# Moving seven of nine feature tiles of an attention gate from TensorE rows to VectorE multiply-adds in a one-core transformer block

## The chip, the core and the metric

The kernel runs on one core of a Trainium2 chip. The metric is the device time of one execution in microseconds (us); lower is better. A core has five engines with a queue of instructions each, which run side by side and wait for one another through semaphores: TensorE (PE, matrix multiplies; PEld is its weight load), VectorE (DVE), ScalarE (ACT), GpSimd (POOL) and SyncE (SP, which here only starts transfers). Transfers between HBM and the on-chip memory SBUF are done by 16 DMA engines. TensorE writes to PSUM, eight banks of 512 f32 values in each of 128 partitions.

## What is computed

One block of a diffusion transformer, on 2 batches of 256 tokens with 1152 features, all in bf16:

```
mod = (silu(c) @ w_mod).reshape(B, 6, 1, D)
shift_a, scale_a, gate_a, shift_m, scale_m, gate_m = [mod[:, i] for i in range(6)]
h = layernorm(x) * (1 + scale_a) + shift_a
q, k, v = (h @ wqkv) split in three, two heads of 576
attn = softmax(q @ k^T * 576 ** -0.5)
a = (attn @ v) @ wo
x = x + gate_a * a
h2 = layernorm(x) * (1 + scale_m) + shift_m
out = x + gate_m * (gelu(h2 @ w_fc1) @ w_fc2)
```

`c` is one vector of 1152 for each batch, so each of the six vectors of `mod` is a product of two rows with a matrix of 1152 x 1152. The change is about `gate_a`, a vector of 1152 for each batch that multiplies the output of the attention projection.

## The kernel before

**Recording and ordering.** The kernel records units of work, each for one engine with an estimated duration (`Sched`, L172), and finds the dependences between them from the memory that they read and write. `schedule` (L281) then fixes the order of each engine's queue with a model of the times. TensorE and SP keep the order in which they were recorded. VectorE, ScalarE and GpSimd take, of the units that the model has ready, the one with the longest path behind it; the first units of VectorE and ScalarE are written out by hand (L909). The order is fixed when the program is built: on the chip an engine waits at the head of its queue, even if what stands behind it is ready.

**Stages.** All 512 tokens lie in SBUF as feature tiles of 128 partitions, KT = 9 of them. TensorE's order is:

- the scale part of `mod` and the K projection (to about 30 us), then `sh` (L887 to L889), the row of `shift_a`
- the last K tile (`proj` to tile 17), and six of nine Q tiles at once, feature tile by feature tile, in PSUM banks 2 to 6 and 1 (L1104 to L1108); the other three Q tiles by `proj` (L871) in banks 0, 1 and 2
- for each batch b and head h, of number idx = 2b + h: the scores in one bank (`s_bank`, L919) and the softmax behind it (`s_and_softmax`, L931): on VectorE `smax` (row maximum, L943), `snb` (L944), `sri` (reciprocal, L949) and `spn` (the normalising multiply, L951), on ScalarE two `sexp` (exponential, L947)
- the V projection in 12 tiles of 128 tokens x 384 features, in banks 0, 1, 2 in turn (`v_proj`, L965). They stand between the score and transpose stages: `PT_b_h` (L953) transposes the probabilities of (b, h) and needs its `spn`; `PT_ev` copies them out of the bank
- `rows` (L977), after the V tile v_2_0: the three vectors `gate_a`, `shift_m` and `scale_m`
- the rest of V, attention times V (`pv`), the output projection `wo_tile` (L1055), the transposes of the second layer norm (`xn2_T`, L1077), and the two MLP matrices to the end

**Row products.** `quad_mm` (L880) has the two rows of silu(c) as weights and streams a weight matrix past them, with the 32-column groups dealt over four parts of the array (q = 0 to 3), so that four matmuls of n columns each stand for 4n columns. `sh` makes nine passes of 288 columns. `rows` makes for each of nine feature tiles one pass of 448 columns into bank 3 and one of 416 into bank 4 (`row_parts`, L975): 27 groups of 32 for each part, 9 for each vector. ScalarE then copies the gate rows to ROWS (`rows_ev`), VectorE transposes the other two vectors (`mt_0`, `mt_1`, L985; `sc1m`, L987), and GpSimd's queue stores the gate in HBM (`st_g0`, `st_g1`) and reads it back to all 128 partitions as GA[b] (`ld_g0`, `ld_g1`, L991). `wo_tile` multiplies by GA[b] (`wo_t1`, VectorE, L1067), adds x on GpSimd (L1068), and goes on to the statistics (L731, L734, L735, L1072) and the normalised tile `xn2` on ScalarE (L1073), which `xn2_T` needs. `wo_tile` and the MLP take the banks 2, 3, 4, 5, 0, 1 in turn.

**The gate of the MLP** is made in another way, late in the kernel, under the MLP's matmuls (`mlp_gate`, L994): VectorE multiplies the weight tile by silu(c), one value for each partition, and adds up over the nine feature tiles (L999 for the first, L1002 for the others); then it sums over the partitions by a 32 x 32 transpose (L1006), a reduction (L1008), three copies (L1011), three additions (L1014), a copy to bf16 (L1016) and a transpose (L1017). GpSimd clears a small tile for it (L1005), stores the result and reads it back to all partitions.

**Loads.** SP's queue holds all weight loads in order: the nine WQ tiles; WV, which overlays the weights of `sh` and so waits for `sh`; the three parts of WMODR (weights of `rows`, three vectors wide, L891); WO; the first two tiles of w_fc1; after the last V tile two more; the weights of the MLP gate (`ld_gm`, into the region O_R); and w_fc2.

**Evictions.** PSUM is copied to SBUF by ScalarE (L681) or VectorE (L683); `qk_evac` (L867) and `v_proj` (L972) take them in turn.

Of the kernel before, what the change touches and what calls it, by code (L numbers as in the profile page):

```python
# [506 lines left out]
CH = 384  # L507
NCH = 3
F0 = 8
KC = 5  # L510
KG = 6


def c_mm(n):
# [7 lines left out]
def c_dve_psum32(n):  # L522
    return 110.0 + 1.13 * n
# [18 lines left out]
def build_kernel(nc, x, c, wqkv, wo, w_mod, w_fc1, w_fc2, out):  # L542
    S = Sched()
# [3 lines left out]
    scratch = scratch_t.ap()  # L547
    with (
# [20 lines left out]
        W1 = 20736  # L569
        O_A, O_B, O_C, O_R = 0, W1, 2 * W1, 3 * W1  # L570
# [25 lines left out]
        WMODR = wmat(O_R + W1, 3 * D)  # L596
# [18 lines left out]
        GA = [sb(O_GA + b * 2304, 2304) for b in range(2)]  # L615
        GM = [sb(o + 18432, 2304) for o in (O_A, O_C)]
        XN2 = [sb(O_R + 4 * W1 - (i + 1) * 2304, 2304) for i in range(4)]
        ROWS = sb(O_R + 4 * W1 - 5 * 2304, 2304)[:, 0:288]
        T1 = [sb(O_X + i * 1536, 1536, F32) for i in range(3)]
        OST = [sb(O_X + 4608 + i * 768, 768) for i in range(3)]  # L620
        gt_offs = ([O_P + i * 1024 for i in range(8)] + [O_B + i * 1024 for i in range(20)]
# [11 lines left out]
        ST32 = sb(misc(72), 72, F32)  # L633
# [4 lines left out]
        MT = sb(misc(2304), 2304, F32)  # L638
# [21 lines left out]
        wmod_v = w_mod.rearrange("(k p) f -> p k f", p=P)  # L660
# [34 lines left out]
        for (ka, kb) in ((0, KC), (KC, KT)):  # L695
            w = (kb - ka) * P
# [49 lines left out]
        for t in range(4):  # L746
# [3 lines left out]
            else:  # L750
# [3 lines left out]
                                                                                 op0=ALU.subtract, op1=ALU.mult),  # L754
# [112 lines left out]
        def qk_evac(j, bank):  # L867
            copy_on("act" if ev_rr[0] % 2 == 0 else "dve", QK[:, j, :], ps32(bank), 512, False, "qk_ev%d" % j)
            ev_rr[0] += 1

        def proj(W, j, dst_j, H, bank):  # L871
            S.unit("pe", KT * c_mm(512), "qk_%d" % dst_j)
            for kt in range(KT):
                mm(ps32(bank), W[:, kt, j * 128:(j + 1) * 128], H[:, kt, :], kt == 0, kt == KT - 1)
            qk_evac(dst_j, bank)

        def quads(w, g0, g1, q):
            return w.rearrange("p (g q c) -> p g q c", q=4, c=32)[:, g0:g1, q, :]
# [8 lines left out]
        S.unit("pe", KT * 4 * 31.0 + 100.0, "sh")  # L887
        for kt in range(KT):
            quad_mm(0, WSH[:, kt, :], 0, 9, kt)  # L889
        dma(WV, wqkv_v[:, :, 2 * D:3 * D], D * D * 2, "ld_wv", run=2304)  # L890
        for k0 in range(0, KT, 3):  # L891
            dma(WMODR[:, k0:k0 + 3, :], wmod_v[:, k0:k0 + 3, 2 * D:5 * D], 3 * P * 3 * D * 2, "ld_modr%d" % k0)
        MT1 = ps32(0, 0, 288)
        dve(c_dve_psum32(288), lambda e: e.transpose(SHA, MT1), [MT1], [SHA], "sha")  # L894
        for kt in range(KT):
            for b in range(2):
                src, dst = HK[:, kt, b * 256:(b + 1) * 256], HX[:, kt, b * 256:(b + 1) * 256]
# [77 lines left out]
        row_parts = ((3, 0, 14), (4, 14, 27))  # L975

        def rows():  # L977
            S.unit("pe", KT * 864 / 2.4 + 500.0, "rows")
# [3 lines left out]
            copy_on("act", ROWS, ps32(3, 0, 288), 288, False, "rows_ev")  # L982
            for i, (bank, c0, n, d0) in enumerate(((3, 288, 160, 0), (4, 0, 416, 160))):
                src, dst = ps32(bank, c0, n), MT[:, d0:d0 + n]
                dve(c_dve_psum32(n), lambda e, src=src, dst=dst: e.transpose(dst, src), [src], [dst], "mt_%d" % i)  # L985
            sc, so = MT[:, 288:576].rearrange("p (k r) -> p k r", r=32)[:, :, 0:2], SC1M.rearrange("p (k b) -> p k b", b=2)
            dve(170, lambda e: e.tensor_scalar(out=so, in0=sc, scalar1=1.0, scalar2=None, op0=ALU.add), [sc], [so], "sc1m")  # L987
            for b in range(2):
                dma(scratch[0, b].rearrange("(k q c) -> q k c", q=4, c=32), ROWS[b:128:32, :].rearrange("p (k c) -> p k c", c=32),
                    2304, "st_g%d" % b, eng="pool")  # L990
            for b in range(2):  # L991
                dma(GA[b], scratch[0, b].partition_broadcast(P), P * D * 2, "ld_g%d" % b, eng="pool")

        def mlp_gate(prev):  # L994
            for b in range(2):
# [117 lines left out]
        s_halves()  # L1113
# [57 lines left out]
        for t in range(4):  # L1171
            b = t // 2
# [69 lines left out]
```

## Time and profile before

| | |
|---|---|
| time, median of 3 runs | 246.3 us (246.1 to 247.2) |
| the profiled execution | 246.26 us, of which the profile's span is 244.2 us and 2.06 us lie around it |
| TensorE busy | 239.3 us (98%) |
| VectorE, ScalarE, GpSimd busy | 98.7 us (40%), 63.0 us (26%), 21.5 us (9%) |
| DMA | 51.57 MB, mean 211 GB/s |
| granted TensorE clock | 1.0 of full speed |

All times in the text are from the start of the span. An "idle before" is the time an engine stood still in front of an instruction, and its releaser is what ended the wait. The lines of the MLP gate, L999 to L1017, are the nearest rows for the operations that the change adds. The timeline merges neighbouring instructions of one line; the start of a merged row is that of its first.

### The profile page before, as it was taken

Reading aid. Unit: us, or ns where it says so; the run is one execution under the profiler, and the core shown is the slowest. Engines: PE = TensorE matmul, PEld = TensorE weight load, DVE = VectorE, ACT = ScalarE, POOL = GpSimd, SP = SyncE. Lnnn points to the kernel's source line nnn. Section 1 sums busy time; section 2 is a strip of 40 time slices with the busy share of each in tenths; the row PEclk is TensorE's granted clock in tenths of the full one; section 3 lists DMA queues with packets and bytes.
Section 4 is the critical chain, followed back from the end, with each engine's and each line's share of the span. In section 5 each row is a group of like instructions: output and inputs, shape, how many; then the busy total and the mean of one; then the engine's idle time right before and its main releaser. Section 6 shows DMA issues by size and latency. Waiting matters only on the chain.

```text
span 244.2 us, 3973 instructions
## 1 busy us (share of the span) xinstructions
PE 239.3 (98%) x1721; PEld 146.8 (60%) x1731; DVE 98.7 (40%) x205; ACT 63.0 (26%) x128; POOL 21.5 (9%) x37
## 2 busy tenths in 40 slices
PE   7999999999999999999999999999999999999995
PEld 2689844466557666798544444444565656566575
DVE  3742450446323689879999600000022222111112
ACT  5730340235312306983322333222000000000000
POOL 1400000000021275600000110000000000000000
DMA  6999999999994999979943589200000000000000
GB/s 244 350 377 393 389 381 401 419 422 406 387 329 111 341 386 391 392 246 396 349 132 101 172 256 393 79 0 3 0 16 16 19 17 16 19 16 16 29 22 16
DMA packets 28875, 51.57 MB, mean 211 GB/s; under 512 B 1587, under 2 KB 15675, under 8 KB 28859
## 3 DMA queue, kind: packets, MB, share of 16 engines
q1 hardware_dynamic: 28384, 50.14, 56.9%
q0 software_dynamic: 448, 1.19, 2.0%
q8 instruction: 13, 0.21, 0.4%
q14 instruction: 3, 0.02, 0.0%
q10 hardware_dynamic: 27, 0.00, 0.0%
HBM read 50.14 MB, written 1.19 MB: 210 GB/s over the span
## 4 chain that ended last, share of the span: by engine, by line
PE 97%; ACT 1%; issue 0%; DVE 0%; POOL 0%; POOLq 0%
PE psum L686 95%; PE psum L689 2%; ACT arena L1091 1%; ACT arena L1073 1%; DVE arena L792 0%; POOL arena L709 0%; DVE arena L1184 0%; DVE arena L1185 0%; POOL arena L708 0%; DVE arena L783 0%; POOL arena L713 0%; POOLq L1227 0%
## 5 line engine op out<-in xcount | busy, mean ns | idle before, releaser
L686 PE MATMUL psum<-arena 128*128 128x384 bf16 (+9 forms) x1632 | 236.1, 312 | 2.2 <-POOL arena L709 1.4
L686 PEld LDWEIGHTS psum<-arena 128*128 128x128 bf16 (+1 forms) x1642 | 141.4, 97 | 92.3 <-issue 5.0
L1184 DVE TENSOR_TENSOR arena<-psum,arena 128x384 f32<-128x384 f32 (+3 forms) x14 | 7.0, 501 | 89.4 <-PE psum L686 89.4
L1101 ACT ACTIVATE arena<-psum 128x512 bf16<-128x512 f32 (+1 forms) x44 | 22.5, 522 | 42.6 <-PE psum L686 42.6
L681 ACT ACTIVATE arena<-psum 128x512 bf16<-128x512 f32 (+6 forms) x28 | 14.8, 549 | 40.1 <-PE psum L686 38.2
L683 DVE CAST arena<-psum 128x512 bf16<-128x512 f32 (+2 forms) x21 | 13.0, 627 | 26.5 <-PE psum L686 26.3
L1002 DVE SCALAR_TENSOR_TENSOR arena<-arena 128x1152 f32<-128x1152 bf16 x16 | 21.3, 1409 | 0.0
L1068 POOL TENSOR_TENSOR arena<-arena 128x384 f32<-128x384 f32 x12 | 11.0, 914 | 12.9 <-DVE arena L1067 11.7
L667 POOL DMA_DIRECT2D dit_scratch<-arena x4 | 2.6, 662 | 94.0 <-ACT arena L681 58.7
L731 DVE BATCH_NORM_STATS2 arena<-arena 128x6 f32<-128x384 f32 (+1 forms) x18 | 9.5, 549 | 1.2 <-DMA arena<-in_x_dram 1.1
L1073 ACT ACTIVATE arena<-arena 128x1152 bf16<-128x1152 f32 x4 | 5.4, 1353 | 9.5 <-DVE arena L1072 9.5
L1067 DVE TENSOR_TENSOR arena<-psum,arena 128x384 f32<-128x384 f32 x12 | 6.6, 548 | 3.2 <-PE psum L686 3.0
L689 PEld LDWEIGHTS psum<-arena 128*128 128x128 bf16 (+1 forms) x89 | 6.0, 98 | 2.4 <-DMA arena<-in_c_dram 0.8
L689 PE MATMUL psum<-arena 128*128 128x128 bf16 (+1 forms) x89 | 7.3, 219 | 0.1
L1185 DVE TENSOR_TENSOR arena<-arena 128x384 bf16<-128x384 f32 (+3 forms) x14 | 7.0, 501 | 0.5
L1091 ACT ACTIVATE arena<-psum,arena 128x128 bf16<-128x128 bf16 x16 | 6.1, 460 | 3.2 <-PE psum L689 2.5
L1088 DVE TENSOR_SCALAR arena<-psum,arena 128x128 bf16<-128x128 bf16 x20 | 5.5, 336 | 2.0 <-PE psum L689 1.8
L943 DVE TENSOR_REDUCE arena<-psum 128x2 f32<-128x512 f32 x4 | 2.8, 692 | 4.0 <-PE psum L686 3.7
L947 ACT ACTIVATE arena<-psum,arena 128x256 bf16<-128x256 f32 x8 | 3.7, 470 | 2.4 <-DVE arena L944 1.9
L735 POOL TENSOR_TENSOR arena<-arena 128x1 f32<-128x1 f32 x6 | 3.3, 555 | 6.1 <-DVE arena L734 6.1
L792 DVE TENSOR_SCALAR arena<-psum,arena 128x256 bf16<-128x256 bf16 x7 | 2.4, 348 | 3.6 <-PE psum L689 2.3
L900 ACT ACTIVATE arena<-arena 128x256 bf16<-128x256 bf16 x6 | 2.5, 495 | 3.3 <-DVE arena L894 3.3
(46 smaller groups left out, 43.1 us busy)
## 6 DMA issues: line engine op xcount, KB each, us to landing
arena<-in_w_mod_dram SPq DMA_DIRECT2D x4, 2592.0 KB, 20.2
arena<-in_w_fc_dram SPq DMA_DIRECT2D x9, 1152.0 KB, 8.2
arena<-in_w_fc_dram SPq DMA_DIRECT2D x4, 2592.0 KB, 17.4
arena<-in_wqkv_dram SPq DMA_DIRECT2D x18, 288.0 KB, 10.2
arena<-in_w_mod_dram SPq DMA_DIRECT2D x3, 864.0 KB, 13.2
arena<-in_wqkv_dram SPq DMA_DIRECT2D x1, 2592.0 KB, 10.9
arena<-in_wo_dram SPq DMA_DIRECT2D x1, 2592.0 KB, 32.7
arena<-in_w_mod_dram SPq DMA_DIRECT2D x3, 480.0 KB, 6.8
```

The source lines that it names most:

```text
L681: act(c_act(n), lambda e: e.activation(out=dst, in_=src, func=ACTF.Copy), [src], [dst], name)
L683: dve(c_dve_psum16(n) if psum16 else c_dve_psum32(n), lambda e: e.tensor_copy(dst, src), [src], [dst], name)
L686: S.instr(lambda e: e.matmul(o, lhsT=l, rhs=r, start=st, stop=sp, **kw), reads=[l, r], writes=[o])
L689: S.instr(lambda e: e.transpose(o, i_, idn), reads=[i_, idn], writes=[o])
L731: dve(550, lambda e, s=s, o=o: e.bn_stats(out=o, in_=s), [s], [o], "bn_%s_%d" % (tag, ci))
L1002: u = dve(1300, lambda e, o=o, w=w, s1=s1: e.scalar_tensor_tensor(out=o, in0=w, scalar=s1, in1=o, op0=ALU.mult, op1=ALU.add), [w, s1, o], ...
L1068: S.op("pool", 930, lambda e, xs=xs, x1c=x1c: e.tensor_tensor(out=x1c, in0=x1c, in1=xs, op=ALU.add), reads=[x1c, xs], writes=[x1c], name=" ...
L1073: act(1344, lambda e: e.activation(out=xn2, in_=x1, func=ACTF.Identity, scale=rs, bias=nm), [x1, rs, nm], [xn2], "xn2_%d" % t)
L1091: act(440, lambda e, o=o, dst=dst, s1=s1, s2=s2: e.activation(out=dst, in_=o, func=ACTF.Identity, scale=s1, bias=s2), [o, s1, s2], [dst], ...
L1101: act(c_act(ntok), lambda e: e.activation(out=dst, in_=o, func=ACTF.Gelu_apprx_tanh), [o], [dst], "gelu_%d_%d" % (f, tok0))
L1184: dve(c_dve_psum32(w), lambda e, o=o, gm=gm, t1=t1: e.tensor_tensor(out=t1, in0=o, in1=gm, op=ALU.mult), [o, gm], [t1], "fc2_t1_%d_%d" % ( ...
L1185: dve(c_dve_32(w), lambda e, t1=t1, x1c=x1c, ost=ost: e.tensor_tensor(out=ost, in0=t1, in1=x1c, op=ALU.add), [t1, x1c], [ost], "fc2_out_%d ...
```

## The change

`gate_a` is split: its first NG = 7 feature tiles of 128 (FG = 896 of 1152 features) are made on VectorE in the way of the MLP gate, and the last two stay in `rows`.

- `rows` makes a pass of 352 and one of 288 columns for each feature tile. ROWS, its copy and its store hold 64 columns for each part, and `mt_0` and `mt_1` are 288 columns each.
- `attn_gate` is recorded before the Q tiles: for each feature tile and batch one multiply or multiply-add of 128 x 896 (2 and 16), two transposes and two reductions of 128 x 896, eight small operations on 32 partitions, a clearing of a small tile on GpSimd, and two stores on GpSimd's queue. Its tiles lie in O_R, where `ld_gm` loads later.
- The gate's part of WMODR is loaded by three transfers of its own, of 672 KB each, ahead of WV; the other three WMODR loads shrink from 2592 to 1920 KB.
- All twelve V evictions, and all nine Q evictions but two (`qk_ev1`, `qk_ev3`), go to ScalarE. Before, ScalarE had six of V and four of Q.

In the order of the built program, VectorE's queue has the 18 multiplies and adds spread from the end of the `hx` operations (L903) to behind the last `spn`: seven ahead of `qk_ev1`, four ahead of the first `smax`, then singly between the softmax operations, and the last two behind `spn_3`, followed by the transposes, `ga_red0`, `mt_0`, `mt_1`, `ga_red1` and the small operations. On ScalarE the eviction `qk_ev8` stands ahead of the first `sexp`, and `v_ev1_0` ahead of the last pair. On GpSimd the clearing of the small tile stands near the start, between the clearing at L713 and the making of the identity (L709); the stores are followed by the two reads `ld_g0` and `ld_g1`. TensorE's order is the same but for the widths in `rows`.

```diff
+NG = 7
+FG = NG * 128
...
-        ROWS = sb(O_R + 4 * W1 - 5 * 2304, 2304)[:, 0:288]
+        ROWS = sb(O_R + 4 * W1 - 5 * 2304, 2304)[:, 0:288 - 32 * NG]
+        ACCA = sb(O_R, FG * 8, F32).rearrange("p (b d) -> p b d", b=2)
+        ACTA = sb(O_R + FG * 8, FG * 8, F32).rearrange("p (b d) -> p b d", b=2)
...
-            qk_evac(dst_j, bank)
+            if dst_j == 17:
+                qk_evac(dst_j, bank)
+            else:
+                copy_on("act", QK[:, dst_j, :], ps32(bank), 512, False, "qk_ev%d" % dst_j)
...
+        for k0 in range(0, KT, 3):
+            dma(WMODR[:, k0:k0 + 3, 0:FG], wmod_v[:, k0:k0 + 3, 2 * D:2 * D + FG], 3 * P * FG * 2, "ld_ga%d" % k0, run=FG * 2)
         dma(WV, wqkv_v[:, :, 2 * D:3 * D], D * D * 2, "ld_wv", run=2304)
         for k0 in range(0, KT, 3):
-            dma(WMODR[:, k0:k0 + 3, :], wmod_v[:, k0:k0 + 3, 2 * D:5 * D], 3 * P * 3 * D * 2, "ld_modr%d" % k0)
+            dma(WMODR[:, k0:k0 + 3, FG:3 * D], wmod_v[:, k0:k0 + 3, 2 * D + FG:5 * D], 3 * P * (3 * D - FG) * 2, "ld_modr%d" % k0)
...
-            copy_on("act" if v_rr[0] % 2 else "dve", V[:, t, ci * CH:(ci + 1) * CH], o, CH, False, "v_ev%d_%d" % (t, ci))
+            copy_on("act", V[:, t, ci * CH:(ci + 1) * CH], o, CH, False, "v_ev%d_%d" % (t, ci))
-        row_parts = ((3, 0, 14), (4, 14, 27))
+        row_parts = ((3, NG, 18), (4, 18, 27))
...
+        def attn_gate():
+            for kt in range(KT):
+                for b in range(2):
+                    o, w, s1 = ACCA[:, b, :], WMODR[:, kt, 0:FG], ST32[:, b * 9 + kt:b * 9 + kt + 1]
+                    if kt == 0:
+                        dve(150 + FG * 0.6, lambda e, o=o, w=w, s1=s1: e.tensor_scalar(out=o, in0=w, scalar1=s1, scalar2=None, op0=ALU.mult),
+                            [w, s1], [o], "ga_%d_%d" % (b, kt))
+                    else:
+                        dve(150 + FG * 1.1, lambda e, o=o, w=w, s1=s1: e.scalar_tensor_tensor(out=o, in0=w, scalar=s1, in1=o, op0=ALU.mult, op1=ALU.add),
+                            [w, s1, o], [o], "ga_%d_%d" % (b, kt))
+            pool(100, lambda e: e.memset(GBA, 0.0), [], [GBA], "gba0")
...
+            for b in range(2):
+                dma(scratch[0, b, 0:FG].rearrange("(g c) -> g c", c=32), GTA[0:4 * NG, 32 * b:32 * b + 32], FG * 2, "st_ga%d" % b, eng="pool")
...
+        attn_gate()
         qb = (2, 3, 4, 5, 6, 1)
...
-        for j in range(KG):
-            qk_evac(j, qb[j])
+        for j, eng in ((5, "act"), (1, "dve"), (2, "act"), (3, "dve"), (4, "act"), (0, "act")):
+            copy_on(eng, QK[:, j, :], ps32(qb[j]), 512, False, "qk_ev%d" % j)
```

More of the change, by code (lines that the diff above doesn't have):

```diff
@@ L971, in v_proj @@
                 mm(o, HX[:, kt, t * 128:(t + 1) * 128], WV[:, kt, ci * CH:(ci + 1) * CH], kt == 0, kt == KT - 1)
-            copy_on("act" if v_rr[0] % 2 else "dve", V[:, t, ci * CH:(ci + 1) * CH], o, CH, False, "v_ev%d_%d" % (t, ci))
-        row_parts = ((3, 0, 14), (4, 14, 27))
+            copy_on("act", V[:, t, ci * CH:(ci + 1) * CH], o, CH, False, "v_ev%d_%d" % (t, ci))
+        row_parts = ((3, NG, 18), (4, 18, 27))
         def rows():
-            S.unit("pe", KT * 864 / 2.4 + 500.0, "rows")
+            S.unit("pe", KT * (864 - 32 * NG) / 2.4 + 500.0, "rows")
             for kt in range(KT):
@@ L981, in rows @@
                     quad_mm(bank, WMODR[:, kt, :], g0, g1, kt)
[L982 to L985, printed above, removed]
+            n = 288 - 32 * NG
+            copy_on("act", ROWS, ps32(3, 0, n), n, False, "rows_ev")
+            for i, (bank, c0) in enumerate(((3, n), (4, 0))):
+                src, dst = ps32(bank, c0, 288), MT[:, i * 288:(i + 1) * 288]
+                dve(c_dve_psum32(288), lambda e, src=src, dst=dst: e.transpose(dst, src), [src], [dst], "mt_%d" % i)
             sc, so = MT[:, 288:576].rearrange("p (k r) -> p k r", r=32)[:, :, 0:2], SC1M.rearrange("p (k b) -> p k b", b=2)
@@ L988, in rows @@
             for b in range(2):
-                dma(scratch[0, b].rearrange("(k q c) -> q k c", q=4, c=32), ROWS[b:128:32, :].rearrange("p (k c) -> p k c", c=32),
-                    2304, "st_g%d" % b, eng="pool")
+                dma(scratch[0, b, FG:D].rearrange("(k q c) -> q k c", q=4, c=32), ROWS[b:128:32, :].rearrange("p (k c) -> p k c", c=32),
+                    2304 - 2 * FG, "st_g%d" % b, eng="pool")
             for b in range(2):
                 dma(GA[b], scratch[0, b].partition_broadcast(P), P * D * 2, "ld_g%d" % b, eng="pool")
+        def attn_gate():
[10 more added lines that the diff above has]
+            for b in range(2):
+                a_, t_ = ACCA[:, b, :], ACTA[:, b, :]
+                dve(150 + FG * 1.1, lambda e, a_=a_, t_=t_: e.transpose(t_, a_), [a_], [t_], "ga_T%d" % b)
+                t3, o = t_.rearrange("p (g r) -> p g r", r=32), GPA[:, 0, b, :]
+                dve(150 + FG * 1.1, lambda e, t3=t3, o=o: e.tensor_reduce(out=o, in_=t3, axis=AX.X, op=ALU.add), [t3], [o], "ga_red%d" % b)
+            gp = GPA.rearrange("p q b g -> p q (b g)")
+            for q in range(1, 4):
+                i_, o_ = gp[32 * q:32 * q + 32, 0, :], gp[0:32, q, :]
+                dve(200, lambda e, i_=i_, o_=o_: e.tensor_copy(o_, i_), [i_], [o_], "ga_mv%d" % q)
+            for a_, b_ in ((0, 1), (2, 3), (0, 2)):
+                x_, y_ = gp[0:32, a_, :], gp[0:32, b_, :]
+                dve(200, lambda e, x_=x_, y_=y_: e.tensor_tensor(out=x_, in0=x_, in1=y_, op=ALU.add), [x_, y_], [x_], "ga_add%d" % b_)
+            g0, gb = GPA[0:32, 0, :, :], GBA.rearrange("p (b g) -> p b g", b=2)[:, :, 0:4 * NG]
+            dve(200, lambda e: e.tensor_copy(gb, g0), [g0], [gb], "ga_bf")
+            dve(200, lambda e: e.transpose(GTA, GBA), [GBA], [GTA], "ga_t")
+            for b in range(2):
+                dma(scratch[0, b, 0:FG].rearrange("(g c) -> g c", c=32), GTA[0:4 * NG, 32 * b:32 * b + 32], FG * 2, "st_ga%d" % b, eng="pool")
```

3 lines of the change are left out of this document (added).

## The prediction

> **What bounds the kernel now.** I read the page's busy line first, then what TensorE waits for, then TensorE's work by shape, then the stretch around the change in the timeline. The page and TensorE's waits:
>
> ```profile
> PE 239.3 (98%) x1721; PEld 146.8 (60%) x1731; DVE 98.7 (40%) x205; ACT 63.0 (26%) x128; POOL 21.5 (9%) x37
> ```
>
> ```profile
> PE psum L686 <- POOL arena L709: 1.4, 1, 1.4
> PE psum L686 <- issue: 0.2, 1, 0.2
> ```
>
> TensorE is busy for 239.3 of 244.2 us, and its only real wait is the 1.4 us for the identity at the start. So the end moves by what is taken from TensorE's queue, less each wait that is put into it. VectorE's 40% is an average: what counts is whether it has room between 35 and 82 us. TensorE's weight loads around the two stages with 2-column weights show what a pass costs:
>
> ```profile
> 29.95 0.96 PEld L686 LDWEIGHTS psum<-arena 128*2 128x2 bf16 x36 [0.21 <-issue]
> 31.16 0.33 PEld L686 LDWEIGHTS psum<-arena 128*128 128x128 bf16 x3 [0.25 <-issue]
> ```
>
> ```profile
> 65.96 3.02 PEld L686 LDWEIGHTS psum<-arena 128*2 128x2 bf16 x72 [0.32 <-issue]
> 69.35 0.60 PEld L686 LDWEIGHTS psum<-arena 128*128 128x128 bf16 x5 [0.37 <-issue]
> ```
>
> The first pair is `sh`: nine passes of 288 columns from 29.95 to 31.16, 1.21 us. The second is `rows`: nine passes of 448 and nine of 416, 7776 columns, from 65.96 to 69.35, 3.39 us.
>
> **What is taken away: rows.** After the change there are nine passes of 352 and nine of 288, 5760 columns, 2016 fewer. If what is not streaming is fixed for a stage, a column costs (3.39 - 1.21) / (7776 - 2592) = 0.42 ns, and 0.85 us go. If it is paid by the pass (18 against 9), 3.39 - 2 x 1.21 = 0.97 us are for 2592 columns, 0.37 ns each, and 0.75 us go. I take the middle, **-0.8 us**. Everything behind `rows` on TensorE moves forward together, as it has no wait there.
>
> **The added VectorE work, and its cover.** The nearest rows by shape, and where VectorE meets TensorE:
>
> ```profile
> L1002 DVE SCALAR_TENSOR_TENSOR arena<-arena 128x1152 f32<-128x1152 bf16 x16 | 21.3, 1409 | 0.0
> ...
> L1006 DVE STREAM_TRANSPOSE arena<-arena 128x2304 f32<-128x2304 f32 x1 | 2.6, 2578 | 0.0
> L1008 DVE TENSOR_REDUCE arena<-arena 128x72 f32<-128x2304 f32 x1 | 2.6, 2553 | 0.0
> ...
> L999 DVE TENSOR_SCALAR arena<-arena 128x1152 f32<-128x1152 bf16 x2 | 1.5, 809 | 0.0
> ```
>
> ```profile
> 50.38 0.69 DVE L943 TENSOR_REDUCE arena<-psum 128x2 f32<-128x512 f32 x1 [2.77 <-PE psum L686]
> ...
> 64.03 0.37 PEld L689 LDWEIGHTS psum<-arena 128*128 128x128 bf16 x4
> ...
> 82.71 0.56 DVE L1067 TENSOR_TENSOR arena<-psum,arena 128x384 f32<-128x384 f32 x1 [0.31 <-PE psum L686]
> ```
>
> The 16 multiply-adds of L1002 overlap: they fill 21.35 us, 1.33 us from start to start. For 896 instead of 1152 elements that is 1.05 us (1.04 in proportion; 1.12 with no overlap, by the slope between 558 ns for the 384-element L1185 and 1409 ns). The plain multiplies start 0.77 us apart, 0.6 us at 896. VectorE's queue then runs so:
>
> - Start: the last WQ load is issued at 25.67 and lands 10.0 us later, at 35.7; WV is issued at 31.47 and lands after 10.9, at 42.4. So WV's 2592 KB took 6.7 us, and a gate load of 672 KB, next in the queue, 1.7 us: the three land near 37.4, 39.2 and 40.9.
> - Two multiplies and five adds from 37.4 end at 43.9, before the Q banks are ready at 44.97. Two evictions of 0.66 end at 46.3, four adds at 50.5. `smax_0` could start at 50.38: 0.1 us late.
> - One add more, then `snb_0` at 52.2 (51.11 before); ScalarE has `qk_ev8` until 52.9 (0.60 from 52.32) ahead of the exponentials anyway, and a pair of them takes 1.0 (59.72 to 60.73). `smax_1` waits for TensorE at 55.53, so VectorE catches up there. Going on with 1.05 for each add and the softmax rows' own 0.15 to 0.69, `spn_0` ends at 55.1, `spn_2` at 58.1, `spn_1` at 60.7. TensorE needs them at 59.0, 60.7 and 62.3: slack 3.9, 2.6, 1.6.
> - `spn_3`: ScalarE evicts v_1_0 from 61.02 and then does the last exponentials, to 62.5; `sri_3` to 62.7; `PT_ev1` cannot start before 62.93 and takes 0.42; `spn_3` takes 0.69 and ends at 64.0. TensorE loads its result at 64.03. This is the one tight place: a wait from nothing to 0.3 us. I take **+0.1**.
>
> Behind `spn_3` come two adds, two transposes (by the slope to 619 ns for 416 elements, 1.1 each), two reductions (1.1 each), two transposes of 288 (0.48, the L894 row), 0.13 for `sc1m` and eight small operations, which took 1.80 (136.60 to 138.40): VectorE is done near 73.4, long before its next eviction at 77.97.
>
> **The gate's way through HBM.** The stores took 1.7 to 4.5 us to land, the reads 4.1 to 7.3 (page part 6 and the DMA view by window). GA[0] then lands between 73.4 + 1.7 + 4.1 = 79.2 and 73.4 + 4.5 + 7.3 = 85.2; before, it was 75.09 + 4.1 = 79.2. The DMA engines are nearly empty from 74 to 76 us (share 0.01), so I expect some 80. `wo_t1` needs it at 82.71 - 0.65 = 82.1. A late gate costs nothing at first: TensorE fills six banks, VectorE has 0.90 + 0.44 + 0.44 + 0.16 us of waits to catch up in, and `xn2_0` ends at 92.98 for a weight load at 94.05, 1.07 more. Only past 85.1 does each us cost one. **0**.
>
> **The other edits.** V and Q evictions on ScalarE take 0.49 and 0.60 against 0.56 and 0.69 on VectorE, and a V tile comes every 1.46 to 1.68 us: cover enough, **0**; without it v_2_0 would wait for bank 0, whose eviction ends at 61.5 for a need at 64.4. WV lands 5.2 us later, at 47.6, for a need at 53.2 (eviction at 54.66 less nine matmuls of 0.16). WMODR's last load lands at 34.90 + 26.5 = 61.4 as before, since the bytes ahead are the same, for a need at 66.0. `ld_gm` now waits for the gate's stores (75 to 78), behind the w_fc1 loads in SP's queue and ahead of w_fc2, which is used after 170 us: **0**.
>
> The clearing on GpSimd lands ahead of the identity, TensorE's one wait. Its like (L1005) took 0.17 us, that at L713 0.10 and starts while L708 still runs: 0 to 0.15 later, of which TensorE's later waits before 12 us may swallow some (a weight load stands 0.23 for a transfer at 10.46). **+0.05**.
>
> **A rule weighed.** The Trainium skill, "DMA: Bandwidth & Descriptors", § Bandwidth, advises batches of at least 1 MiB for 75% of peak, against this cut, and § Anatomy of one DMA fits 2.0 us plus bytes over 436 GB/s to one transfer of GpSimd's queue. By it, as an estimate, the three gate loads would take 10.7 us instead of 5.2. The trace speaks against it on SP's queue: the nine WQ loads of 288 KB land at 390 GB/s, as fast as the large ones. What it would do is the third rival.
>
> **Sum.** Against the profiled execution of 246.26 us (its span 244.2 and 2.06 around it; the median is 246.3, so the two may be taken as one): 246.26 - 0.8 + 0.1 + 0.05 = **245.6 us**, a span of 243.6. What a measurement of this kernel can tell from no change is about 0.5%, 1.2 us; my -0.65 is within it.
>
> **Rivals.**
> 1. *The softmax takes the gain back.* VectorE has some 20 changes of operation between 44.97 and 64 us; if each costs 0.05 to 0.1 more for a semaphore than its row shows, `spn_3` is 0.4 to 1.2 late past its slack. For: the 0.0 us of slack there. Against: the waits at 55.53 and 62.93 let VectorE catch up. 245.6 + 0.4 to 1.2: **246.0 to 246.8**. 0.14.
> 2. *The gate lands late, and the time ends above before.* The place is `wo_t1`, the point 85.1 us. The longest store and read give 85.2; if VectorE's tail (27 instructions behind `smax_0`) is also 2.5 us late, 87.7, 2.6 past the point: 245.6 + 2.6 = **248.2**. The old time is passed from 85.8. For: both transfers in series after VectorE's last operation. Against: empty DMA engines at that moment. 0.07.
> 3. *The cut loads leave gaps.* WMODR's last part lands at 61.4 plus the gaps and is needed at 66.0, WV at 47.6 plus the gaps for 53.2; gaps of 5.6 us cost 1.0: **246.6**. Against: no such gap behind the WQ loads. 0.03.
> 4. *The rows do not shrink*, because the 36 narrower pairs of load and matmul are bound by issue: 72 weight loads filled 3.02 us. Against: in `sh` 36 filled 0.96. 246.26 + 0.15, **246.4**. 0.05.
>
> My forecast has 0.69; 0.02 are left for something faster that I do not see.
>
> **Range and chances.** The forecast's own range is 245.2 to 246.0 (wait 0 to 0.3, columns 0.75 to 0.85, start 0 to 0.15, and the spread of the runs, 246.1 to 247.2). To hold 8 in 10 it must take in rivals 1, 3 and 4: 245.1 to 246.9. Faster by over 0.5% (below 245.0): 0.03. Slower by over 0.5% (above 247.5): rival 2 and a tail, 0.08. Within: 0.89.
>
> **What would show it.** `rows`: first to next weight load 2.5 to 2.65 us. Softmax: TensorE's weight load of PT_1_1 with no wait, or one of up to 0.3 with L951 as releaser. Gate: the second pair of stores issued near 73.4, the reads landing before 82, L1067 still released by TensorE. Start: the first matmul at 1.42 to 1.57. I am wrong if TensorE shows waits above 0.5 us between 44 and 100 us, or if VectorE's adds are much longer than 1.05 us apart where nothing stands between them.

## The result, and the profile after

Against the kernel before, run beside it on the same chip, the changed kernel takes **0.9952 [0.9941, 0.9964]** of the time: medians of eleven runs each, 245.35 us (244.78 to 245.97) and 246.71 us (246.1 to 247.51). By this ratio it is 1.2 us less (0.9 to 1.5); the two medians lie 1.36 apart, because this set of the kernel before lies high (its later medians are 246.3 to 246.4). The forecast was 245.6 us in a range of 245.1 to 246.9, a gain of 0.65. The time has two parts: the median span is 243.6 us, where the forecast had 243.6 and the kernel before has 244.3 to 244.4; what lies around the span is 1.75 us, where the kernel before has 2.07 (2.05 to 2.07).

The busy line of the changed kernel's page:

```profile
PE 238.6 (98%) x1721; PEld 146.7 (60%) x1731; DVE 116.8 (48%) x226; ACT 67.0 (27%) x137; POOL 22.4 (9%) x40
```

VectorE has 18.1 us more to do, ScalarE 4.0, TensorE 0.7 less. What TensorE waits for (total, times, longest, in us):

```profile
PE psum L693 <- POOL arena L716: 1.5, 1, 1.5
PE psum L696 <- DMA arena<-in_c_dram: 0.6, 1, 0.6
PE psum L693 <- issue: 0.2, 1, 0.2
```

The second line is new and is no term of the sum: the vector c landed late in this execution. That is why its span is 244.2 us, that of the profile of before, though the median is 0.7 below. Four of the profiles of the experiments, e3, e6_4us, e7 and e11, show c late too (2.73 to 3.07 us), the others do not (2.38 to 2.54, but for e8, where c is loaded behind other work); whether the change has a part in that is not shown. The place is the weight load of c's transpose at the start. Before:

```profile
2.38 0.10 PEld L689 LDWEIGHTS psum<-arena 18*128 18x128 bf16 x1 [0.84 <-DMA arena<-in_c_dram]
```

After:

```profile
3.15 0.10 PEld L696 LDWEIGHTS psum<-arena 18*128 18x128 bf16 x1 [1.54 <-DMA arena<-in_c_dram]
```

It is 0.77 us late at c, 0.75 at the next stage (8.76 for 8.01), and 0.82 at `rows`. To compare the two profiles ahead of `rows`, 0.82 us are to be taken off the times of the changed kernel. The timeline of the changed kernel from the multiply-adds to the stage behind `rows` (start, duration, engine, line, operation, shapes; in brackets the idle time before it and what ended it):

```profile
38.36 5.40 DVE L1015 SCALAR_TENSOR_TENSOR arena<-arena 128x896 f32<-128x896 bf16 x5
...
51.24 0.68 DVE L955 TENSOR_REDUCE arena<-psum 128x2 f32<-128x512 f32 x1
...
64.08 0.68 DVE L963 TENSOR_TENSOR arena<-arena 128x512 bf16<-128x512 bf16 x1
...
64.84 0.37 PEld L696 LDWEIGHTS psum<-arena 128*128 128x128 bf16 x4
...
66.78 2.27 PEld L693 LDWEIGHTS psum<-arena 128*2 128x2 bf16 x72 [0.32 <-issue]
...
69.33 24.63 PEld L693 LDWEIGHTS psum<-arena 128*128 128x128 bf16 x166 [0.28 <-issue]
```

`rows` begins at 66.78 and the next stage at 69.33: 2.55 us for 3.39. Before, they began at 65.96 and 69.35. So the stage gives back what the late c cost, and from there both profiles show the same times to within 0.03 us. From the start of `rows` to the end of the span it is 178.24 us before and 177.42 after. In the second line, 51.24 less 0.82 is 50.42: the first softmax row starts 0.04 later than before, though the multiply-adds stand ahead of it in VectorE's queue. The tight place holds: the last normalised row, L963, ends at 64.76, and TensorE's load of its transpose follows at 64.84 with no wait in brackets. The margin is only 0.08 us.

The groups of the added VectorE work (count, busy us, mean ns of one, idle before):

```profile
L1015 DVE SCALAR_TENSOR_TENSOR arena<-arena 128x896 f32<-128x896 bf16 x16 | 17.6, 1145 | 0.0
...
L1020 DVE STREAM_TRANSPOSE arena<-arena 128x896 f32<-128x896 f32 x2 | 2.1, 1086 | 0.0
L1022 DVE TENSOR_REDUCE arena<-arena 128x28 f32<-128x896 f32 x2 | 2.1, 1043 | 0.0
```

Five adds that follow one another without a break fill 5.40 us, from 38.36 on: less the 1.145 us of the last, that is 1.06 from start to start for the 1.05 of the forecast. The gate's way through HBM, in the same timeline:

```profile
73.79 1.09 POOL L674 DMA_DIRECT2D dit_scratch<-arena  x2 [2.31 <-DVE arena L1032]
...
76.04 1.02 SPq L674 DMA_DIRECT2D arena<-in_w_fc_dram  x2
...
76.39 1.12 POOL L674 DMA_DIRECT2D arena<-dit_scratch  x2 [1.51 <-DMA dit_scratch<-arena]
...
83.28 0.56 DVE L1109 TENSOR_TENSOR arena<-psum,arena 128x384 f32<-128x384 f32 x1 [0.91 <-DMA arena<-dit_scratch]
...
94.02 0.65 PEld L696 LDWEIGHTS psum<-arena 128*128 128x128 bf16 x9
```

The second pair of stores is issued at 73.79, the reads at 76.39, 2.6 us later, and the gate is there 6.9 us after that, at 83.28. VectorE stands idle for 0.91 us ahead of its first user, L1109; 0.31 of these it waited for TensorE in the kernel before too, so the gate is 0.6 us late. TensorE shows no wait behind it: the lateness is swallowed.

### The profile page after: what moved, and what is told of

Its sections match the earlier page's. It is cut to its first block, busy times and chain, and to the rows that moved or that the text cites. A ratio compares the mean times of both kernels' runs of the same rounds, so it can differ in the third digit from the quotient of the medians.

```text
span 244.2 us, 4012 instructions
## 1 busy us (share of the span) xinstructions
PE 238.6 (98%) x1721; PEld 146.7 (60%) x1731; DVE 116.8 (48%) x226; ACT 67.0 (27%) x137; POOL 22.4 (9%) x40
## 4 chain that ended last, share of the span: by engine, by line
PE 96%; ACT 1%; DMA 1%; DVE 0%; issue 0%
PE psum L693 94%; PE psum L696 2%; DMA arena<-in_c_dram 1%; ACT arena L1133 1%; ACT arena L1115 1%; DVE arena L799 0%; DVE arena L1227 0%; DVE arena L1228 0%; DVE arena L790 0%
## 5 line engine op out<-in xcount | busy, mean ns | idle before, releaser
L693 PE MATMUL psum<-arena 128*128 128x384 bf16 (+8 forms) x1632 | 235.3, 310 | 2.2 <-POOL arena L716 1.5
L688 ACT ACTIVATE arena<-psum 128x512 bf16<-128x512 f32 (+6 forms) x37 | 18.9, 539 | 38.4 <-PE psum L693 38.4
L1015 DVE SCALAR_TENSOR_TENSOR arena<-arena 128x896 f32<-128x896 bf16 x16 | 17.6, 1145 | 0.0
L690 DVE CAST arena<-psum 128x512 bf16<-128x512 f32 (+1 forms) x12 | 7.7, 647 | 13.3 <-PE psum L693 13.2
L674 POOL DMA_DIRECT2D dit_scratch<-arena x6 | 3.6, 606 | 96.1 <-ACT arena L688 58.5
L1109 DVE TENSOR_TENSOR arena<-psum,arena 128x384 f32<-128x384 f32 x12 | 6.6, 548 | 2.9 <-PE psum L693 1.8
```

What stands on the lines that cost most here:

```text
L693: S.instr(lambda e: e.matmul(o, lhsT=l, rhs=r, start=st, stop=sp, **kw), reads=[l, r], writes=[o])
L1015: dve(150 + FG * 1.1, lambda e, o=o, w=w, s1=s1: e.scalar_tensor_tensor(out=o, in0=w, scalar=s1, in1=o, op0=ALU.mult, op1=ALU.add), [w, s1 ...
```

## The experiments

My theory: the narrower `rows` alone makes the change of the span, the rest is covered, and the cover of the gate ends at one point, some 3 us past its need. The rivals: the evictions give the gain; the added VectorE work takes something back; the cut loads or the clearing move the start; and, for the cover, that the point lies elsewhere or that lateness past it costs something other than one for one. Times are medians, ratios are to the kernel before with 95% intervals, "around" is the time less the span.

| run | ratio | time | span | around |
|---|---|---|---|---|
| before | | 246.3 to 246.7 | 244.3 to 244.4 | 2.07 |
| after | 0.9952 [0.9941, 0.9964] | 245.35 | 243.6 | 1.75 |
| e1_rows | 0.9968 [0.9957, 0.9979] | 245.58 | 243.6 | 2.07 |
| e2_evict | 0.9997 [0.9989, 1.0006] | 246.33 | 244.2 | 2.09 |
| e3_fullrows | 0.9991 [0.9982, 1.0] | 246.19 | 244.4 | 1.75 |
| e4_clear_late | 0.9949 [0.9937, 0.9961] | 245.07 | 243.3 | 1.76 |
| e5_loads | 0.9993 [0.998, 1.0006] | 246.05 | 244.15 | 1.81 |
| e8_c_later | 0.9955 [0.9939, 0.9971] | 245.23 | 243.5 | 1.74 |
| e6_gate_2us | 1.0009 [1.0, 1.0019] | 246.58 | 244.9 | 1.75 |
| e6_gate_4us | 1.0187 [1.0157, 1.0216] | 250.68 | 248.95 | 1.77 |
| e7_ng8 | 1.0248 [1.0229, 1.0266] | 252.44 | 250.7 | 1.75 |
| e10_gate_sp | 0.9959 [0.9946, 0.9973] | 245.29 | 243.5 | 1.72 |
| e11_ng8_sp | 0.9951 [0.9935, 0.9967] | 245.14 | 243.4 | 1.74 |
| e12_split | 0.9991 [0.9982, 1.0] | 246.15 | 244.25 | 1.83 |

### e1_rows: the narrow rows alone

The kernel before, with `rows` cut and nothing put in its place: the seven tiles of the attention gate are left out, and the store sends other data in their stead.

```diff
-        row_parts = ((3, 0, 14), (4, 14, 27))
+        row_parts = ((3, NG, 18), (4, 18, 27))
...
+                dma(scratch[0, b:b + 1, 0:FG], X[b:b + 1, 0, 0:FG], 2 * FG, "st_ga%d" % b, eng="pool")
```

> The kernel before with the narrow rows alone: no multiply-adds, no cut loads, evictions as before. The first seven tiles of the attention gate are left out (values of x stand in for them). Rows theory: 5760 instead of 7776 columns take 0.85 us out of TensorE's queue and nothing else matters, so the time is 0.85 us below before, and the first to next weight load of rows is 2.55 us. Rival (part of the measured -1.2 us comes from the evictions, the loads or the start): no more than -0.85 here, while one of the other runs shows the rest of about 0.4.

Measured: 0.9968 [0.9957, 0.9979], span 243.6. TensorE's weight loads:

```profile
65.88 2.27 PEld L688 LDWEIGHTS psum<-arena 128*2 128x2 bf16 x72 [0.32 <-issue]
68.42 2.55 PEld L688 LDWEIGHTS psum<-arena 128*128 128x128 bf16 x17 [0.28 <-issue]
```

2.54 us, as in the full change. The narrow rows alone give the whole 0.7 to 0.8 of the span; around it nothing moves (2.07).

### e2_evict: the evictions alone

```diff
-            copy_on("act" if v_rr[0] % 2 else "dve", V[:, t, ci * CH:(ci + 1) * CH], o, CH, False, "v_ev%d_%d" % (t, ci))
+            copy_on("act", V[:, t, ci * CH:(ci + 1) * CH], o, CH, False, "v_ev%d_%d" % (t, ci))
...
-            qk_evac(j, qb[j])
+            copy_on(eng, QK[:, j, :], ps32(qb[j]), 512, False, "qk_ev%d" % j)
```

> The kernel before with the evictions of the change alone (all of V, seven of nine Q tiles on ScalarE). Rows theory: no change, 0 within 0.2 us, since TensorE waits for no eviction either way. Rival (evictions give part of the gain): -0.3 to -0.5 us.

Measured: 0.9997 [0.9989, 1.0006], span 244.2, and `rows` as before:

```profile
65.86 3.02 PEld L686 LDWEIGHTS psum<-arena 128*2 128x2 bf16 x72 [0.32 <-issue]
69.25 1.74 PEld L686 LDWEIGHTS psum<-arena 128*128 128x128 bf16 x12 [0.37 <-issue]
```

The evictions are worth nothing by themselves. They make room on VectorE.

### e3_fullrows: everything but the narrow rows

The gate's seven tiles are computed on VectorE, and TensorE computes them as well; the rows' own result for them is not stored.

```diff
-        row_parts = ((3, NG, 18), (4, 18, 27))
+        row_parts = ((3, 0, 14), (4, 14, 27))
```

> The changed kernel with rows at their full width again: VectorE makes seven tiles of the gate, the rows make them too, and those of the rows are not used. Rows theory: the added VectorE work, the cut loads and the evictions are all hidden, so the time is that of before, 0 to +0.15 us. Rival (something else in the change gains): 0.3 to 0.5 us below before. Rival (the added work costs): above before by more than 0.3 us, with a wait of TensorE for L963 or for an eviction.

Measured: 0.9991 [0.9982, 1.0], span 244.4, that of the kernel before. The tight place in its timeline, and `rows`:

```profile
63.49 0.68 DVE L963 TENSOR_TENSOR arena<-arena 128x512 bf16<-128x512 bf16 x1
...
64.25 0.37 PEld L696 LDWEIGHTS psum<-arena 128*128 128x128 bf16 x4
66.19 3.02 PEld L693 LDWEIGHTS psum<-arena 128*2 128x2 bf16 x72 [0.32 <-issue]
69.57 1.42 PEld L693 LDWEIGHTS psum<-arena 128*128 128x128 bf16 x10 [0.37 <-issue]
```

The last row ends at 64.17, its load follows at 64.25 with no wait. So 18 us more on VectorE cost nothing in the span. What is left, some 0.25 us of the time that I had not expected (0 to 0.15 more), lies around it.

### e4_clear_late and e8_c_later: the start

e4 is the changed kernel with the clearing behind the identity on GpSimd; e8 is e4 with two of fifteen warm-up matmuls ahead of c's transpose.

```diff
+             "pool": ["ones", "nhalf", "ident"],
```

```diff
+        for i in range(2):
+            S.unit("pe", 215.0, "warm_b0_%d" % i)
+            mm(ps32(2), IDENT, Q4B, True, True)
...
-        warm(15, "b")
+        warm(13, "b")
```

> The changed kernel with the clearing of the gate's small tile behind the identity in GpSimd's queue instead of ahead of it. Rows theory: the first matmul starts at 1.42 instead of 1.48 us, and the time is 0 to 0.1 us below the changed kernel's, so 0.9 to 1.3 us below before. Rival (the place of the clearing moves the start in a way that gains): 0.3 us or more above the changed kernel's, so about 0.85 below before or less.

> The changed kernel with the clearing behind the identity, and the transpose of c behind two of the fifteen warm-up matmuls, so that a late c (2.4 to 3.2 us in the profiles) no longer holds the warm-ups. Start theory: the spread of the runs comes from the start (c and x landing, and when the clock rises), so the upper runs come down: the span's spread narrows from 1.2 to about 0.8 us and its median is 0 to 0.3 us below the changed kernel's 243.6. Rival (c is not what sets the spread): the same spread and median as with the clearing moved alone, 243.3.

Measured: 0.9949 [0.9937, 0.9961] and 0.9955 [0.9939, 0.9971]. In e4 the first matmul is at 1.41 (1.48 after, 1.42 before) and c's load at 2.38. Its five runs lie between 244.96 and 245.29, inside the 244.78 to 245.97 of the changed kernel, and the intervals overlap: a cost of the clearing of 0.1 us can be neither shown nor excluded. That the early clearing makes the changed kernel's runs spread wider than e4's is refuted by e10_gate_sp (below), which also clears late: nine runs, 244.87 to 246.12. The kernel before spreads as widely (1.0 to 1.4 us in each set). e8 was meant to fill the wait for c; in its profile c's load waited 0.83 us all the same, and the time is no better than e4's. Its six spans lie within 0.3 us, but so do e4's five, so the narrower spread that I expected is not shown either. What sets the spread of the start stays open.

### e5_loads and e12_split: the cut loads

e5 is the kernel before with the three gate loads cut off and put ahead of WV; e12 makes the same cut and leaves the pieces in the old place.

```diff
+        for k0 in range(0, KT, 3):
+            dma(WMODR[:, k0:k0 + 3, 0:FG], wmod_v[:, k0:k0 + 3, 2 * D:2 * D + FG], 3 * P * FG * 2, "ld_ga%d" % k0, run=FG * 2)
...
-            dma(WMODR[:, k0:k0 + 3, :], wmod_v[:, k0:k0 + 3, 2 * D:5 * D], 3 * P * 3 * D * 2, "ld_modr%d" % k0)
+            dma(WMODR[:, k0:k0 + 3, FG:3 * D], wmod_v[:, k0:k0 + 3, 2 * D + FG:5 * D], 3 * P * (3 * D - FG) * 2, "ld_modr%d" % k0)
```

> The kernel before with the cut loads of the change alone: three gate loads of 672 KB ahead of WV, the other three of 1920 KB, rows and evictions as before. The kernels with the gate on VectorE showed 1.75 us around the span where before has 2.07; this tells whether the cut loads bring that. Span theory: the span stays at 244.3 within 0.2, WV and WMODR land in time, TensorE does not wait for them. Around the span: 1.75 us if the three more entries in SP's queue make the difference, 2.07 if it is VectorE's or GpSimd's part. Rival (gaps between cut loads): a wait of TensorE at v_0_0 or rows.

> The kernel before with each of the three WMODR loads split in two (672 and 1920 KB) in their old place behind WV: three more entries in SP's queue, no other order. If the number of entries is what takes 0.3 us from the time around the span, it is 1.75 to 1.8 here too (before: 2.07); if it is their place ahead of WV, 2.07. The span stays at 244.3 within 0.2 either way.

Measured: 0.9993 [0.998, 1.0006] and 0.9991 [0.9982, 1.0]; spans 244.15 and 244.25, and no wait of TensorE for WV or WMODR. The cut is free in the span. But around the span it takes 0.24 to 0.26 us off (1.81 and 1.83 for 2.07), whether the pieces are moved or not. So most of the 0.32 us that the whole change gains around the span goes with the three more entries in SP's queue, not with their order. Why, the profile cannot show: it has nothing outside the span. The other 0.07 us are open too. Nor is 2.07 fixed for the kernel before: of its 70 runs beside the experiments, ten have 1.70 to 1.79 around the span and the others 1.88 to 2.21; all eleven of the changed kernel have 1.69 to 1.80. So the change makes a value the rule that the kernel before shows now and then.

### e6_gate_2us, e6_gate_4us and e7_ng8: the gate made late

In e6 each large transpose at the end of VectorE's gate work is done two or three times over, for 2.2 or 4.5 us more (the line below is that of e6_gate_2us); nothing else changes. e7 computes eight tiles on VectorE instead of seven.

```diff
+                for r in range(1):
+                    S.instr(lambda e, a_=a_, t_=t_: e.transpose(t_, a_), [a_], [t_], "ga_T%d" % b)
```

```diff
-NG = 7
+NG = 8
```

> The changed kernel with each of the gate's two large transposes done three times over, in the same order of the queues: VectorE's tail is 4.2 us longer and the gate arrives that much later, at about 87.4 us for a need at 82.4. By the prediction's account a late gate is free for 3.0 us (1.9 of waits to catch up in and 1.1 ahead of xn2_T), then costs one for one: 2.0 us above the changed kernel, 1.5 to 2.5. Rival (TensorE's six banks cover it all): no change. Rival (no cover): 4 us or more.

> The changed kernel with eight of nine tiles of the gate on VectorE (1024 elements). Rows theory: 288 columns less, 0.12 us below the changed kernel in TensorE's span from rows on, with the stage at 2.43 us. VectorE's adds are 1.19 us apart; the order moves more of them behind spn_3, so the softmax holds and the gate arrives near 84, inside its free 3 us. In all -0.1 us against the changed kernel, too little for the timed runs. Rival (cover is used up): a wait of TensorE of 0.3 us or more for L963 or at xn2_T.

> The changed kernel with each of the gate's two large transposes done twice: VectorE's tail is 2.1 us longer. Linear account: stores at 75.9, gate at 85.4 for a need at 82.4, just inside the 2.9 us that the 4 us run and the run with eight tiles showed to be free: 0 to 0.5 us above the changed kernel. Queue account: what costs is being behind SP's next loads (w_fc1, issued at 76.0 when the last V tile is done); stores at 75.9 and above all the reads behind them then meet full DMA queues, as with 4 us (stores 5.2, reads 6.9 to landing), the gate comes at 87 to 88, and the run is 2 to 3.5 us above the changed kernel.

Measured: 1.0009 [1.0, 1.0019], 1.0187 [1.0157, 1.0216] and 1.0248 [1.0229, 1.0266]. None of the three came as expected. Against the changed kernel I expected 0.1 us less of e7 and got 7 more, 2.0 us more of e6_gate_4us and got 5.3; e6_gate_2us, with 1.3 us more, lies between its two accounts (0 to 0.5, and 2 to 3.5). Timeline of e6_gate_2us:

```profile
75.23 1.08 POOL L674 DMA_DIRECT2D dit_scratch<-arena  x2 [4.50 <-DVE arena L1034]
75.29 1.02 SPq L674 DMA_DIRECT2D arena<-in_w_fc_dram  x2
...
79.26 0.57 POOL L674 DMA_DIRECT2D arena<-dit_scratch  x1 [2.95 <-DMA dit_scratch<-arena]
...
85.31 1.02 DVE L1111 TENSOR_TENSOR arena<-psum,arena 128x384 f32<-128x384 f32 x2 [3.69 <-PE psum L693]
...
94.03 0.50 PEld L696 LDWEIGHTS psum<-arena 128*128 128x128 bf16 x9 [0.82 <-ACT arena L1117]
```

Of e6_gate_4us:

```profile
75.85 1.02 SPq L674 DMA_DIRECT2D arena<-in_w_fc_dram  x2
...
78.08 1.08 POOL L674 DMA_DIRECT2D dit_scratch<-arena  x2 [6.79 <-DVE arena L1034]
...
83.78 1.26 POOL L674 DMA_DIRECT2D arena<-dit_scratch  x2 [4.62 <-DMA dit_scratch<-arena]
...
89.64 1.02 DVE L1111 TENSOR_TENSOR arena<-psum,arena 128x384 f32<-128x384 f32 x2 [7.45 <-PE psum L693]
...
98.35 0.88 PEld L696 LDWEIGHTS psum<-arena 128*128 128x128 bf16 x9 [3.93 <-ACT arena L1117]
```

Of e7_ng8:

```profile
75.40 1.02 SPq L674 DMA_DIRECT2D arena<-in_w_fc_dram  x2
...
76.78 1.03 POOL L674 DMA_DIRECT2D dit_scratch<-arena  x2 [5.89 <-DVE arena L1032]
...
83.07 1.11 POOL L674 DMA_DIRECT2D arena<-dit_scratch  x2 [5.26 <-DMA dit_scratch<-arena]
...
90.58 1.02 DVE L1109 TENSOR_TENSOR arena<-psum,arena 128x384 f32<-128x384 f32 x2 [8.85 <-DMA arena<-dit_scratch]
...
99.30 0.65 PEld L696 LDWEIGHTS psum<-arena 128*128 128x128 bf16 x9 [3.93 <-ACT arena L1115]
```

Two of the three gate users name TensorE as releaser, though they stood idle for 3.69 and 7.45 us, and TensorE's part took 0.31 of it wherever the gate was in time: the late reads are what held them. In e6_gate_2us the reads are not issued together: the line shows the first, for the gate of batch 0, and the second follows at 81.83, when its own store is in. Each line's own numbers give the account. "Idle" is VectorE's idle time ahead of the gate's first user; "late" is the last weight load, `xn2_T`, less 94.02 us of the changed kernel, which is first shifted by each run's own start of `rows` (66.78 after; 66.03, 66.60 and 66.27 here, and 0.13 for the narrower rows of e7); the cost is the median span less 243.6.

| run | stores to reads | reads to gate | idle | late | idle - late | cost |
|---|---|---|---|---|---|---|
| after | 2.60 | 6.89 | 0.91 | 0 | | 0 |
| e6_gate_2us | 4.03 | 6.05 | 3.69 | 0.76 | 2.93 | 1.3 |
| e6_gate_4us | 5.70 | 5.86 | 7.45 | 4.51 | 2.94 | 5.35 |
| e7_ng8 | 6.29 | 7.51 | 8.85 | 5.92 | 2.93 | 7.1 |

Three runs agree on the point: 2.93 us of idle time are free, or 2.6 us of lateness behind the 0.31 for TensorE. Past it, a us of the gate's lateness costs more than a us, and lateness of VectorE does not pass on to the gate one for one: the stores leave 2.2, 4.5 and 3.6 us later than after (each less its shift), and the gate comes 2.8, 6.5 and 7.9 us later. The cause stands in the first two lines of each fence, the stores and SP's loads. In the changed kernel the stores go out 2.25 us ahead of SP's second pair of w_fc1 loads, in the late ones together with them or behind them, and the small transfers take 4.0 to 6.3 us instead of 2.6. The reads stand behind these loads in the changed kernel already. The Trainium skill says in "Trainium Kernel Development and Optimization", § Key Constraints, that transfers issued by SP, ScalarE and GpSimd all run on the same 16 DMA engines and interleave; the trace agrees: a queue of its own on GpSimd does not keep 1.8 KB stores clear of SP's loads.

A second part comes after the wait. Windows of e7_ng8 (us, busy time of TensorE, its weight loads, VectorE, ScalarE and GpSimd with the number of instructions, granted TensorE clock, DMA share, GB/s):

```profile
96.00:98.00 2.00, 0.00 (x0) 0.00 (x0) 1.96 (x4) 0.10 (x1) 1.96 (x4) 1.00 1.06 393
98.00:100.00 2.00, 0.70 (x9) 0.70 (x10) 1.97 (x7) 1.25 (x1) 1.35 (x2) 0.90 1.05 388
100.00:102.00 2.00, 2.00 (x9) 0.99 (x8) 1.95 (x6) 1.25 (x4) 1.86 (x3) 0.50 1.06 394
102.00:104.00 2.00, 2.00 (x11) 1.09 (x10) 1.91 (x6) 1.95 (x3) 0.16 (x1) 0.75 1.05 391
```

TensorE's own rows there, from these transposes to the next, and those of the changed kernel:

```profile
99.30 0.91 PE L696 MATMUL psum<-arena 128*128 128x128 bf16 x9 [3.54 <-ACT arena L1115]
100.00 4.57 PE L693 MATMUL psum<-arena 128*128 128x384 bf16 x18
104.41 0.67 PE L696 MATMUL psum<-arena 128*128 128x128 bf16 x9
```

```profile
94.18 0.67 PE L696 MATMUL psum<-arena 128*128 128x128 bf16 x9
94.69 3.09 PE L693 MATMUL psum<-arena 128*128 128x384 bf16 x18
97.61 0.93 PE L696 MATMUL psum<-arena 128*128 128x128 bf16 x9
```

TensorE stands still for 3.5 us, and the granted clock falls to 0.50 and is back at about 103 us; the 18 matmuls take 4.57 us for 3.09. In e6_gate_4us the same wait of 3.5 us brings the same 0.50; in e6_gate_2us, whose waits there are 0.2 to 0.5 us, the clock stays at 1.00. That accounts for the cost. By TensorE's rows the transposes begin 5.8 us late in e7 and 4.4 in e6_gate_4us (a wait of 1.9 and 0.5 us for a free bank ahead of them included). From them to the next transposes, 3.43 us in the changed kernel, it takes 1.7 and 1.3 us longer, and a wait of 0.26 us at those, which the changed kernel has, is gone: 7.2 and 5.4 for the measured 7.1 and 5.35. In e6_gate_2us it is 0.6 late and 0.8 for further waits, 1.4 for 1.3. The Trainium skill, "TensorE: Matmul & The Clock Gate", Part 1, has the array at half rate after an idle window of about 3.4 us and at full rate again after as long a busy one; these three runs agree with it.

### e10_gate_sp and e11_ng8_sp: the gate ahead of the loads

e10 is e4 with the gate's stores and reads in SP's queue, ahead of the second pair of w_fc1 loads; e11 is e10 with eight tiles.

```diff
-                    2304 - 2 * FG, "st_g%d" % b, eng="pool")
+                    2304 - 2 * FG, "st_g%d" % b)
...
-                dma(GA[b], scratch[0, b].partition_broadcast(P), P * D * 2, "ld_g%d" % b, eng="pool")
+                dma(GA[b], scratch[0, b].partition_broadcast(P), P * D * 2, "ld_g%d" % b)
...
+        gate_io()
```

> The changed kernel with the clearing behind the identity, and the gate's four stores and two reads in SP's queue ahead of the second pair of w_fc1 loads, which then wait for the gate. Queue account: with no weight load in front of them the stores land in about 2 us and the reads in 3 to 4, so GA[0] is there by 80, L1067's counterpart waits for TensorE and not for the DMA; the loads behind start 2 to 3 us later, which no one waits for. Time as with the clearing alone, 245.1 (span 243.3), 0 within 0.2.

> The run before with eight tiles of the gate on VectorE instead of seven. With the transfers from GpSimd's queue eight tiles cost 7 us. Queue account: here the stores go ahead of the loads, the gate lands near 82 to 83, inside the free 2.9 us, and the narrower rows give their 0.12 us: 0.1 us below the run before. Linear account (the gate is late because VectorE is): still 4 us or more above it.

Measured: 0.9959 [0.9946, 0.9973] and 0.9951 [0.9935, 0.9967]. Timeline of e11_ng8_sp:

```profile
76.08 0.82 SPq L674 DMA_DIRECT2D dit_scratch<-arena  x2
...
77.52 0.82 SPq L674 DMA_DIRECT2D arena<-dit_scratch  x2
78.39 1.07 SPq L674 DMA_DIRECT2D arena<-in_w_fc_dram  x2
...
81.62 0.56 DVE L1112 TENSOR_TENSOR arena<-psum,arena 128x384 f32<-128x384 f32 x1 [0.31 <-PE psum L693]
...
92.95 0.65 PEld L696 LDWEIGHTS psum<-arena 128*128 128x128 bf16 x9
```

The stores leave 0.3 us earlier than in e7 (76.08 and 76.78, with `rows` at 65.83 and 66.27), are back in 1.4 us instead of 6.3, and the multiply waits for TensorE again, by 0.31 us as in the kernel before; so it does in e10. All 7 us of e7 are gone. It is the order of the transfers that made eight tiles dear. SP's queue as such does not make them fast: the second stores leave at 73.79 in the changed kernel and at 73.69 in e10, both while the last of the earlier loads still moves (DMA share 0.63 and 0.48 from 73 to 74 us), and they take 2.6 us from GpSimd's queue and 2.8 from SP's. In e11 they find the DMA engines idle (share at most 0.01 from 75 to 77 us). The reads land after 3.7 and 4.0 us in e10 and e11, ahead of SP's loads, and after 5.8 to 7.4 behind them. The eighth tile's own gain, 0.13 us of `rows`, is less than these runs can tell: e11 is not measurably faster than the changed kernel, and neither is e10.

## Why the prediction was right, point by point

- **Rows, -0.8 (0.75 to 0.85).** Right: 2.55 us for 3.39 in the profile, 2.54 in e1; 0.84 over 2016 columns is 0.42 ns each, the fixed-stage reading. e1 shows that this term is the change of the span.
- **`spn_3`, +0.1 (0 to 0.3).** The queue came out as worked through: 64.0 forecast, 64.76 less 0.82 = 63.94 found. It costs 0, not 0.1, in the changed kernel and in e3. The adds came 1.06 apart for 1.05.
- **Clearing, +0.05.** The first matmul is 0.06 later (1.48 for 1.42). That it reaches the end is not shown.
- **"2.06 around it".** This step failed: I took the time around the span as a constant, and it fell to 1.75. With the span of 243.6 that makes 245.35, a quarter us under the forecast. It brings the gain to just under what I had named as the bound of no change. e5 and e12 tie some 0.25 of it to three more loads; why these do it stays open.
- **The sum.** The gain is 1.2 us (0.9 to 1.5) where I forecast 0.65: 0.15 of costs that did not show, and 0.3 around the span that I had not looked for. That the time itself came out within a quarter us is partly luck, since I started from an execution of 246.26 and the kernel before took 246.71 beside the changed one. The 1.2 us that I named as the least that can be told was too coarse: the interval reaches 0.3 us to either side.
- **Gate, 0.** The cost was right, one sign of it wrong: I expected reads landing before 82 and L1109 still released by TensorE. VectorE was done even a little early (73.49 less 0.82 for 73.4), the store took 2.6 us, but the reads took 6.9, in my bounds and above the 4.1 that my "some 80" used. I had looked at the DMA engines from 74 to 76 us; the reads go out later, 0.35 us after SP's loads. The 0.65 us that I took off for the need has no row: the reads land 6.8 us after their issue and L1109 starts 0.1 later. The gate was 0.6 us late of the 2.6 that are free.
- **Rival 1, the softmax:** refuted by e3 (span 244.4, no wait). **Rival 3, the cut loads:** refuted by e5 and e12. The gaps weighed in the forecast would have cost 1 us there; the 672 KB loads cost nothing in the span. **Rival 4:** refuted by the 2.55 us.
- **Rival 2, the gate.** It did not happen, and was rightly placed: free allowance 3.0 forecast, 2.6 measured. Its price was too low. With VectorE 2.5 us late I had 2.6 past the point, one us for one; 3.6 us late cost 7.1 in e7. I had bounded store and read by rows of before, 4.5 and 7.3, and called the DMA engines empty. What was missing is that lateness itself carries the stores into SP's next loads, 6.3 us in e7, that the reads stand behind these loads in any case, 7.5 us there, and that TensorE comes back from a wait of 3.5 us at half clock.

## What to carry to other kernels

- Where TensorE is busy for 98% of the span, work it by its queue: what is taken out of it is the gain, and 18 us more on an engine at 40% cost nothing as long as each result comes before TensorE's load of it. So follow the other engine's queue from one such meeting to the next; its average says little.
- When a result has to go through HBM late on a path, price the transfers by what will be in the DMA queues if it is late, not by what is there now, and issue them ahead of the large loads, in one queue with them. Then try the next step of the same change: here stores that leave 2.2 us later cost 1.3 us and 3.6 us later 7 us, which the time of the changed kernel does not show.

## What the runs showed of the hardware that was not expected

- The time around the span is not a constant of the chip: in the median 2.05 to 2.09 us before, in e1 and in e2; 1.81 and 1.83 with three loads cut in two; 1.72 to 1.77 with the whole change; and ten of 70 runs of the kernel before show 1.70 to 1.79. Its cause is open.
- Issued beside or behind large loads, two stores of 1.8 or 2 KB took 4.0 to 6.3 us until the first read could go out; 2.6 and 2.8 at the end of earlier loads, from GpSimd's queue and from SP's; 1.4 on idle DMA engines.
- Independent multiply-adds on VectorE overlap: 1145 ns long, 1.06 us from start to start (38.36, 39.42, 40.49, 41.55 us).
